# The down weights and the copy of x to the output in 26 small transfers instead of two large ones

## The chip, the cores and the metric

One core of one Trainium2 chip runs the kernel. The metric is the device time of one execution in microseconds; several runs are given by their median. The core has five engines with programs of their own: TensorE (PE, with its weight loads as PEld), VectorE (DVE), ScalarE (ACT), GpSimd (POOL) and SyncE (SP). SP and POOL issue the DMA transfers of this kernel; 16 DMA engines carry them out.

## The reference, cut to what matters

```python
xn = layernorm(x)                            # x: 2048 x 640, bf16
qkv = xn @ wqkv                              # 32 heads of 20
s = (softmax(q k^T / sqrt(20)) v) @ wo       # all 2048 x 2048 scores of each head
g = silu((sigmoid(xn @ w_gate) * (xn @ w_up)) @ w_down)   # 640 -> 1728 -> 640
out = x + s * g
```

The attention branch needs 32 x 2048 x 2048 exponentials. The gated branch is three matrix products with a hidden width of 1728 (13 tiles of 128 columns and one of 64).

## The kernel before, in words

**Setup (L160 to L361).** x is loaded, normalised and transposed into `xnT`; the first tiles of K, Q and V are made.

**Main loop (L1194 to L1246).** The queries go in NQC = 4 chunks of 512, the heads in NG = 8 groups of 4. A pass is one chunk with one group; there are 32. A pass has PER_PASS = 64 banks: a bank is 128 keys of one head against the 512 queries, one score matmul (L1035) of 512 columns. ACT takes the exponentials of two or three banks at once (`act_exp`, L1058); a fourth bank of a round can go to DVE, which builds the exponential by a cubic (`dve_exp`, L1069 to L1082). The products with V (L1167) gather in the PSUM tile `oacc`.

**The order of the work** is not found on the chip. The Python program keeps a clock `pe[0]` and estimated clocks of ACT and DVE, and writes the instructions in the order in which these say they should go. Each engine then takes its instructions in that order and waits on semaphores where an input is not there. `front()` is the first bank not yet issued on some lane.

**Fillers.** Between the rounds PE does the rest of the work in small jobs, sorted by a due bank (L829 to L861) and at most two in flight (L927): Q, K and V products, gate and up products (`gateup_job`, one for each of the 14 hidden tiles and each chunk), down products (`down_job`, 4 for each chunk, which read the weights `wd`, here `glu[1]`, and end in a silu), output products (`out_job`, 4 for each of the first three chunks) and the last chunk's (`part_job`). A job yields "known" (a condition tested while the program is written), "wait", "bank" (a PSUM bank) or "mm". Where there is room and no job, PE multiplies by zeros (L1146).

**Denominators.** At the end of each pass `normalise` copies `oacc` with DVE (L770), and POOL writes the four rows of sums to DRAM (L771) and reads them back over 128 partitions (L776). DVE takes the reciprocal (L780), POOL writes it (L781) and reads it back spread (L787), and DVE multiplies (L799). These small transfers are issued by POOL.

**Transfers on SP.** SP carries the weights of the gate and up products (L619, L621; two buffers each, one load of 160 KB each for a job), the projected Q on its way to DRAM and back (L550, L588, L608), the output weights in 32 small pieces (`load_wo`), and what the change is about: `start_glu` (L878), which runs once the K and V jobs are done and their weights' memory is free. It opens the memory for the gated branch, loads the first gate and up weights, then `wd` (L886, and L887 for the last 64 rows), then copies the first 12 of the 16 row tiles of x to the output in DRAM (L889). `out_job` later adds its result to that copy with an accumulating DMA of POOL (L726).

Of the kernel before, what the change touches and what calls it, by code (L numbers as in the profile page):

```python
# [15 lines left out]
P = 128  # L16
HEAD = 32
GH = 4
NG = HEAD // GH
QC = 512  # L20
# [24 lines left out]
def kernel(  # L45
# [11 lines left out]
    nc = tc.nc  # L57
# [6 lines left out]
    F = B_w_gate.shape[1]  # L64
    NFT = (F + P - 1) // P
    fsz_list = [min(P, F - i * P) for i in range(NFT)]
    TT = S // P
    NQC = S // QC
# [6 lines left out]
    x_view = x2.rearrange("(p t) d -> p t d", t=TT)  # L75
    out_view = out2.rearrange("(p t) d -> p t d", t=TT)
# [296 lines left out]
    DMA_WAIT, LANDED = 3400.0, 4000.0  # L373
# [36 lines left out]
    pe = [0.0]  # L410
# [254 lines left out]

    def down_job(tt):
        c, t4 = divmod(tt, QC // P)
        yield "known", lambda: (len(h_cells.get(c, [])) == NFT and (tt < 2 or tt - 2 in gq_cells)
                                and (c < NQC - 1 or front() >= PER_PASS * (NG * c + t4 + 1)))
        yield "wait", h_cells[c] + ([gq_cells[tt - 2]] if tt > 1 else [])  # L670
        hT = hTs[c]
        d2 = glu[0].tile([P, D], FP32, tag="d2", bufs=2, name="d2")
        got = []
        for h in range(2):
            e0_, e1_ = h * HALF, (h + 1) * HALF
            held, psd = yield "bank",
            for kf in range(NFT):
                fsz = fsz_list[kf]
                nc.tensor.matmul(psd[:, 0:HALF], lhsT=hT[0:fsz, kf, t4 * P:(t4 + 1) * P],  # L679
                                 rhs=glu[1][0:fsz, kf, e0_:e1_], start=(kf == 0), stop=(kf == NFT - 1))  # L680
                yield "mm", MM3
            got.append(dve.add(400.0, [Cell(pe[0] + PE_OUT)], lambda psd=psd, e0_=e0_, e1_=e1_:
                               nc.vector.tensor_copy(out=d2[:, e0_:e1_], in_=psd[:, 0:HALF]), 1))
            give_bank(held, got[-1])
        d_cells.setdefault(c, []).append(Cell(pe[0]))
        made = {}

        def tanh():
            made["t"] = glu[0].tile([P, D], BF16, tag="td", bufs=1, name="td")
            nc.scalar.activation(out=made["t"], in_=d2, func=ACT.Tanh, scale=0.25)  # L690

        def finish():
            last = c == NQC - 1
            gq = kT_all[:, t4, :].bitcast(FP32)[:, 0:D] if last else d2
            nc.vector.scalar_tensor_tensor(out=gq, in0=made["t"], scalar=1.0, in1=d2, op0=ALU.add, op1=ALU.mult)
            if last:
                gq_last[t4] = gq
            else:
                nc.gpsimd.dma_start(out=gq_dram[tt, :, :], in_=d2)

        turned = act.add(590.0, got + td_free[-1:], tanh, 0, EXP_LAG)
        td_free.append(dve.add(740.0, [turned], finish, 2))
        gq_cells[tt] = td_free[-1]
# [2 lines left out]

    def out_job(tt):
        qc, t4 = divmod(tt, QC // P)
        yield "known", lambda: all((qc, g) in ot_cells for g in range(NG)) and (not tt or tt - 1 in out_cells)
        yield "wait", [ot_cells[qc, g] for g in range(NG)] + ([out_cells[tt - 1]] if tt else [])  # L710
        gqr = glu[0].tile([P, D], FP32, tag="gqr", bufs=4, name="gqr")
        nc.sync.dma_start(out=gqr, in_=gq_dram[tt, :, :])
        landed = Cell(pe[0] + 3000.0)
        for h in range(2):
            held, pss = yield "bank",
            for g in range(NG):
                nc.tensor.matmul(pss[:, 0:HALF], lhsT=oTs[qc, g][:, t4 * P:(t4 + 1) * P],  # L717
                                 rhs=wo_pad[:, g, h * HALF:(h + 1) * HALF], start=(g == 0), stop=(g == NG - 1))
                yield "mm", MM3

            def finish(h=h, pss=pss):
                half = gqr[:, h * HALF:(h + 1) * HALF]
                nc.vector.scalar_tensor_tensor(out=half, in0=pss[:, 0:HALF], scalar=0.25, in1=half,
                                               op0=ALU.mult, op1=ALU.mult)
                if h == 1:
                    nc.gpsimd.dma_start(out=out_view[:, tt, :], in_=gqr, accum_op=ALU.add)  # L726

            done = dve.add(400.0, [Cell(pe[0] + PE_OUT), landed], finish, 1)
            give_bank(held, done)
        out_cells[tt] = done  # L730
# [80 lines left out]
    K_COST, B_COST = 5 * MM5, 0.3 * MM5  # L811
    GU_COST, DOWN_COST = 10 * MM5, 2 * NFT * MM3
    OUT_COST, PART_COST = 2 * NG * MM3, 2 * (NG - 2) * MM3
    WO_FROM = 2
    K_DUE, Q_DUE, B_DUE, V_DUE, OUT_DUE = -60, -50, -36, 6, 4 * PER_PASS

    class Job:
# [45 lines left out]
    glu = []  # L863
# [6 lines left out]
    def load_wo():  # L870
        if next_wo[0] == HEAD or front() < PER_PASS * WO_FROM + 8 * next_wo[0]:
            return
        h = next_wo[0]
        g, j = divmod(h, GH)
        nc.sync.dma_start(out=wo_pad[32 * j + 1:32 * j + 1 + Dh, g, :], in_=A_wo[h * Dh:(h + 1) * Dh, :])
        next_wo[0] += 1

    def start_glu():  # L878
        early.close()
        gp = ctx.enter_context(tc.tile_pool(name="glu", bufs=2, side="right", reuse_waits="tile"))  # L880
        wd = gp.tile([P, NFT, D], BF16, tag="wd", bufs=1, name="wd")
        glu.extend([gp, wd])
        for kf in range(WB - 1):
            load_glu(0, kf)
        nf = F // P
        nc.sync.dma_start(out=wd[:, 0:nf, :], in_=B_w_down[0:nf * P, :].rearrange("(f p) d -> p f d", p=P))  # L886
        nc.sync.dma_start(out=wd[0:F - nf * P, nf, :], in_=B_w_down[nf * P:F, :])  # L887
        ahead_of = (NQC - 1) * QC // P
        nc.sync.dma_start(out=out_view[:, 0:ahead_of, :], in_=x_view[:, 0:ahead_of, :])  # L889

    flight = []

# [100 lines left out]
    def front():  # L993
        return min(bank_of(j) for j in range(GH))
# [199 lines left out]
    while pv_pass[0] < len(steps):  # L1194
        advance(pe[0])
        pads()
        load_wo()
        ci, b0 = chunk[0], at_bank[0]
        p = min(b0, NB - 1) // PER_PASS
        until, stuck, can = 1e18, False, False  # L1200
        if b0 < NB:
            wanted = lacks()
            late = [w[2] for w in wanted if w[0].get(w[1]) is None]
            if late:
                must_fill(max(min(late) - 1, 0))
                continue
            cells = [w[0][w[1]] for w in wanted] + [sets[ci % 2]]
            stuck = any(c.t is None for task in act.queue for c in task[3])
            guess = pe[0] + (2000.0 if stuck else 400.0)
            free = max(c.t if c.t is not None else guess for c in cells)  # L1210
            dry = max(act.t, pe[0]) + sum(t[2] for t in act.queue) - MM5 - PE_OUT + 2000.0 * stuck
            into = 0.0 if mode[0] == "score" else INTO["score"]
            until = max(free, dry - AHEAD) - into
            can = all(c.t is not None for c in cells) and free <= pe[0] + into + 1.0
            if can and (until <= pe[0] + (0.0 if mode[0] == "score" else 40.0) or idle):
                idle = False
                n = issue()
                credit = min(credit + n * per_bank(b0), 3000.0)
                continue
        room = until - pe[0]  # L1220
        next_round[0] = until
        held = sum(len(q) for q in ready_p)
        batch = pv_batch()
        cost = PV_TIME + (INTO["pv"] if mode[0] != "pv" else 0.0)
        if batch and (cost <= room or held >= HELD):
            pv(batch)
            idle = False
            continue
        least = (0.0 if mode[0] == "fill" else INTO["fill"]) + MM3
        hurry = (b0 >= NB or stuck or any(x.due < b0 + URGENT for x in flight + jobs[:1])  # L1230
                 or held >= 12 and lacks_v())
        if (credit > 0.0 or hurry) and least <= room:
            took = fill(p, room)
            if took:
                credit -= took
                idle = False
                continue
        if b0 < NB and can and not idle:
            idle = True
            continue  # L1240
        if zero_add(room):
            idle = False
            continue
        soon = [q[k][1].made.t for q in ready_p for k in range(min(2, len(q)))]
        times = [until, pe[0] + 150.0] + [t + SEM for t in soon if t is not None]
        pe[0] = min(t for t in times if t > pe[0] + 1.0)  # L1246
# [83 lines left out]
```

## Time and profile before

| what | value |
|---|---|
| runs | 903.64, 906.02, 906.61 us (median 906.02) |
| profiled execution | 904.48 us |
| its span in the profile | 902.7 us |
| ACT busy | 871.1 us (96%) |
| DVE busy | 840.9 us (93%) |
| PE busy | 824.4 us (91%) |
| POOL busy | 162.2 us (18%) |
| DMA traffic | 64.38 MB, mean 71 GB/s |
| large transfers | `wd` 2080.0 KB and 80.0 KB, x to output 1920.0 KB, one each |

The span is the stretch that the profile covers, from the first to the last instruction; the execution's own time lies 1.8 us above it. A line of the profile's groups reads: line, engine, operation, written tile <- read tiles, shapes, count, busy time and mean of one, and the idle time of the engine just before with what ended most of it. In a timeline row the start and the length come first, and the idle time before stands in brackets at the end. In a row of stretches each engine's busy time has its count of instructions in brackets; behind the engines come the clock that TensorE was granted (1.00 is full), the mean busy share of the DMA engines and what they moved. Landing is the time from the issue of a DMA to the arrival of its last data.

### The profile page before, as it was taken

How to read it: one execution, taken by the hardware profiler on the slowest of the kernel's cores; microseconds unless marked ns; L12 is line 12 of the kernel's file. 1: busy time of each engine (PE TensorE's matmuls, PEld its weight loads, DVE VectorE, ACT ScalarE, POOL GpSimd, SP SyncE). 2: the span in 40 equal slices, each digit the busy share in tenths (PEclk: the TensorE clock that was granted, in tenths of full speed). 3: DMA queues.
4: the chain of work that ended last, by engine and by line, in shares of the span. 5: the costliest groups of instructions: out<-in, count | busy, mean ns of one | idle time of the engine just before them, and what ended most of it. 6: DMA issues, size and time to landing. Idle time of an engine off the chain costs nothing.

```text
span 902.7 us, 16725 instructions
## 1 busy us (share of the span) xinstructions
PE 824.4 (91%) x6190; PEld 288.9 (32%) x6190; DVE 840.9 (93%) x1484; ACT 871.1 (96%) x837; POOL 162.2 (18%) x305
## 2 busy tenths in 40 slices
PE   5899999989999999999999999999999999999995
PEld 3334333322223333232233332232332322233332
DVE  7799999989999999997999999999999989899994
ACT  6999999998999999999999999999999999999992
POOL 7401111101111212111101221101121221011120
PEclk9999999998999999999999999999999999999997
DMA  8112231255321134323202343303022432200021
GB/s 314 45 40 83 71 100 35 65 191 139 72 70 41 55 92 68 70 58 72 63 23 78 88 70 69 75 23 81 27 70 65 106 63 66 56 19 13 13 58 44
DMA packets 105895, 64.38 MB, mean 71 GB/s; under 512 B 79982, under 2 KB 100002, under 8 KB 105594
## 3 DMA queue, kind: packets, MB, share of 16 engines
q1 hardware_dynamic: 95606, 47.21, 19.3%
q0 software_dynamic: 10208, 16.11, 8.0%
q8 instruction: 48, 0.79, 0.4%
q14 instruction: 33, 0.27, 0.1%
HBM read 50.45 MB, written 16.13 MB: 74 GB/s over the span
## 4 chain that ended last, share of the span: by engine, by line
ACT 62%; issue 18%; PE 11%; DVE 7%; DMA 1%; SPq 0%; POOL 0%; DVEq 0%; ACTq 0%; POOLq 0%
ACT p L1058 57%; PE sc L1035 4%; ACT tnh L650 3%; PE oacc L1167 2%; DVE dy L1069 1%; PE work L643 1%; DVE du L1074 1%; PE work L123 1%; PE work L679 1%; ACT td L690 1%; DVE stats L226 1%; PE work L656 1%; DMA den<-den_dram 1%; DVE p L1082 1%; DVE du L1078 1%
## 5 line engine op out<-in xcount | busy, mean ns | idle before, releaser
L1058 ACT ACTIVATE p<-sc 128x1536 bf16<-128x1536 f32 x717 | 828.2, 1357 | 6.4 <-PE spare L1035 2.4
L1035 PE MATMUL sc<-qT,kT_all 21*128 21x512 bf16 x1791 | 280.5, 383 | 49.2 <-ACT p L1058 42.3
L1069 DVE TENSOR_SCALAR dy<-spare 128x512 f32<-128x512 f32 x257 | 175.9, 685 | 24.0 <-PE spare L1035 21.2
L1035 PEld LDWEIGHTS <-kT_all 21*128 21x128 bf16 x2048 | 90.1, 91 | 289.2 <-issue 277.5
L1078 DVE SCALAR_TENSOR_TENSOR du<-du,dy 128x512 f32<-128x512 f32 x257 | 174.7, 683 | 1.6
L1082 DVE SCALAR_TENSOR_TENSOR p<-du,dy 128x512 uint16<-128x512 f32 x257 | 174.5, 682 | 1.3
L1074 DVE SCALAR_TENSOR_TENSOR du<-dy 128x512 f32<-128x512 uint16 x257 | 174.8, 684 | 0.8
L1167 PE MATMUL oacc<-p,v_all 128*21 128x512 bf16 x2048 | 157.8, 385 | 0.3 <-DVE v_all L156 0.3
L1035 PE MATMUL spare<-qT,kT_all 21*128 21x512 bf16 x257 | 99.0, 385 | 2.4 <-DVE row L584 2.4
L771 POOL DMA_DIRECT2D den_dram<-oev x31 | 18.0, 580 | 389.6 <-DVE oev L770 389.6
L679 PE MATMUL work<-wd,hT 128*128 128x320 bf16 x448 | 85.5, 302 | 0.1
L643 PE MATMUL work<-xnT,wg 128*128 128x512 bf16 (+1 forms) x280 | 81.2, 383 | 0.4
L656 PE MATMUL work<-xnT,wu 128*128 128x512 bf16 (+1 forms) x280 | 76.1, 385 | 0.4
L1146 PE MATMUL oacc<-xnT,zero 128*128 128x512 bf16 x227 | 75.2, 384 | 0.6 <-DVE oev L770 0.6
L787 POOL DMA_DIRECT2D rl<-rec_dram x124 | 61.7, 503 | 62.9 <-DMA rec_dram<-den 53.4
L679 PEld LDWEIGHTS <-hT 128*128 128x128 bf16 x448 | 35.0, 97 | 48.6 <-issue 39.1
L1167 PEld LDWEIGHTS <-v_all 128*21 128x21 bf16 x2048 | 29.4, 90 | 65.1 <-issue 63.5
L650 ACT ACTIVATE tnh<-work 128x512 bf16<-128x512 f32 (+1 forms) x56 | 41.1, 733 | 0.0
L660 DVE SCALAR_TENSOR_TENSOR hT<-tnh,work 128x512 bf16<-128x512 bf16 (+1 forms) x56 | 38.0, 679 | 2.6 <-ACT tnh L650 1.9
L781 POOL DMA_DIRECT2D rec_dram<-den x31 | 17.0, 548 | 124.9 <-DVE den L780 120.4
L717 PE MATMUL work<-wo_pad,oT 128*128 128x320 bf16 x192 | 35.6, 302 | 0.0
L643 PEld LDWEIGHTS <-wg 128*128 128x128 bf16 (+1 forms) x280 | 21.7, 98 | 43.0 <-issue 32.2
(111 smaller groups left out, 553.9 us busy)
## 6 DMA issues: line engine op xcount, KB each, us to landing
wg<-in_B_w_gate_dram SPq DMA_DIRECT2D x52, 160.0 KB
wu<-in_B_w_up_dram SPq DMA_DIRECT2D x52, 160.0 KB
rl<-rec_dram POOLq DMA_DIRECT2D x124, 64.0 KB, 2.4
qT<-q_dram SPq DMA_DIRECT2D x31, 128.0 KB
gq_dram<-d POOLq DMA_DIRECT2D x12, 320.0 KB, 2.5
gqr<-gq_dram SPq DMA_DIRECT2D x12, 320.0 KB
kT_all<-k_dram SPq DMA_DIRECT2D x28, 128.0 KB
wd<-in_B_w_down_dram SPq DMA_DIRECT2D x1, 2080.0 KB
```

The lines of the kernel that those rows point to most:

```text
L643: nc.tensor.matmul(psg[0:fsz, :], lhsT=wg[:, kd, 0:fsz], rhs=xnT[:, kd, cols], start=(kd == 0), stop=(kd == KD - 1))
L650: nc.scalar.activation(out=made["t"][0:fsz, :], in_=psg[0:fsz, :], func=ACT.Tanh, scale=0.5)
L656: nc.tensor.matmul(psu[0:fsz, :], lhsT=wu[:, kd, 0:fsz], rhs=xnT[:, kd, cols], start=(kd == 0), stop=(kd == KD - 1))
L679: nc.tensor.matmul(psd[:, 0:HALF], lhsT=hT[0:fsz, kf, t4 * P:(t4 + 1) * P], rhs=glu[1][0:fsz, kf, e0_:e1_], start=(kf == 0), stop=(kf == N ...
L1035: nc.tensor.matmul(ps, lhsT=kT_all[32 * j:32 * j + 1 + Dh, g, kt * P:(kt + 1) * P], rhs=qTs[qc, g][32 * j:32 * j + 1 + Dh, :], start=True, ...
L1058: nc.scalar.activation(out=buf.tile(), in_=ps, func=ACT.Exp, bias=EXP_BIAS, scale=exp_scale)
L1069: nc.vector.tensor_scalar(out=t["y"], in0=ps, scalar1=LEAST, scalar2=None, op0=ALU.max)
L1074: nc.vector.scalar_tensor_tensor(out=t["u"], in0=t["f"], scalar=CUBE_2, in1=t["f"], op0=ALU.add, op1=ALU.mult)
L1078: nc.vector.scalar_tensor_tensor(out=t["u"], in0=t["u"], scalar=CUBE_1, in1=t["f"], op0=ALU.add, op1=ALU.mult)
L1082: nc.vector.scalar_tensor_tensor(out=buf.tile()[:, 0, :].bitcast(U16), in0=t["u"], scalar=CUBE_SCALE, in1=t["y"], op0=ALU.mult, op1=ALU.add)
L1146: nc.tensor.matmul(oacc, lhsT=zero, rhs=xnT[:, 0, 0:QC], start=not begun, stop=not begun, skip_group_check=True)
L1167: nc.tensor.matmul(oacc[32 * j:32 * j + 1 + Dh, :], lhsT=v_all[:, b % PER_PASS // GH, GH * g + j, 0:1 + Dh], rhs=buf.ap[:, i, :], start=(n ...
```

## The change

`start_glu` still loads the first gate and up weights, and then only notes how far the scores are. A new function, called once in each turn of the main loop, issues one transfer whenever `front()` has moved on by six banks: first the 14 tiles of the down weights, one by one (160 KB, the last 80), then 12 row tiles of x to the output (160 KB each). The first down job is not begun before all 14 tiles are issued and the last of these transfers, of either kind, is 4000 ns old by the program's clock; an output job is not begun before its row tile's copy is issued.

```diff
     def down_job(tt):
-        yield "known", lambda: (len(h_cells.get(c, [])) == NFT and (tt < 2 or tt - 2 in gq_cells)
+        yield "known", lambda: (bulk[0] == NFT and pe[0] > bulk_t[0] + LANDED and len(h_cells.get(c, [])) == NFT and (tt < 2 or tt - 2 in gq_cells)
                                 and (c < NQC - 1 or front() >= PER_PASS * (NG * c + t4 + 1)))
...
     def out_job(tt):
-        yield "known", lambda: all((qc, g) in ot_cells for g in range(NG)) and (not tt or tt - 1 in out_cells)
+        yield "known", lambda: (bulk[1] > tt and all((qc, g) in ot_cells for g in range(NG))
+                                and (not tt or tt - 1 in out_cells))
...
-    WO_FROM = 2
+    WO_FROM, BULK_EVERY, bulk_t = 2, 6, [0.0]
...
         for kf in range(WB - 1):
             load_glu(0, kf)
-        nf = F // P
-        nc.sync.dma_start(out=wd[:, 0:nf, :], in_=B_w_down[0:nf * P, :].rearrange("(f p) d -> p f d", p=P))
-        nc.sync.dma_start(out=wd[0:F - nf * P, nf, :], in_=B_w_down[nf * P:F, :])
-        ahead_of = (NQC - 1) * QC // P
-        nc.sync.dma_start(out=out_view[:, 0:ahead_of, :], in_=x_view[:, 0:ahead_of, :])
+        glu_from.append(front())
+
+    glu_from, bulk = [], [0, 0]
+    XT = (NQC - 1) * QC // P
+
+    def load_bulk():
+        if not glu_from or sum(bulk) == NFT + XT or front() < glu_from[0] + BULK_EVERY * (1 + sum(bulk)):
+            return
+        if bulk[0] < NFT:
+            kf = bulk[0]
+            fsz = fsz_list[kf]
+            nc.sync.dma_start(out=glu[1][0:fsz, kf, :], in_=B_w_down[kf * P:kf * P + fsz, :])
+            bulk[0] += 1
+        else:
+            tt = bulk[1]
+            nc.sync.dma_start(out=out_view[:, tt, :], in_=x_view[:, tt, :])
+            bulk[1] += 1
+        bulk_t[0] = pe[0]
...
         load_wo()
+        load_bulk()
```

## The prediction on record

> **What bounds the kernel now.** I read the page first, for the engine that is never free, then its time by stretches, then the one stretch that stands out.
>
> ```profile
> span 902.7 us, 16725 instructions
> ...
> ACT 62%; issue 18%; PE 11%; DVE 7%; DMA 1%; SPq 0%; POOL 0%; DVEq 0%; ACTq 0%; POOLq 0%
> ...
> L1058 ACT ACTIVATE p<-sc 128x1536 bf16<-128x1536 f32 x717 | 828.2, 1357 | 6.4 <-PE spare L1035 2.4
> L1035 PE MATMUL sc<-qT,kT_all 21*128 21x512 bf16 x1791 | 280.5, 383 | 49.2 <-ACT p L1058 42.3
> ```
>
> ACT leads the chain that ended last, and its exponentials at L1058 fill 828.2 of 902.7 us. The order of work on each engine is fixed when the program is written, so an idle microsecond of ACT is a microsecond of the span unless ACT idles later anyway. PE waits for ACT (42.3 us in front of L1035), not ACT for PE. So I look for ACT's idle time. The columns behind the width of a stretch are PE, PEld, DVE, ACT and POOL busy, then granted clock, DMA share, GB/s.
>
> ```profile
> 168.00:196.00 28.00, 26.47 (x196) 8.89 (x198) 27.20 (x51) 28.00 (x26) 3.74 (x8) 1.00 0.33 94
> 196.00:224.00 28.00, 24.93 (x158) 6.80 (x156) 22.88 (x41) 23.62 (x23) 3.63 (x7) 0.88 0.66 205
> 224.00:252.00 28.00, 25.93 (x186) 8.05 (x184) 25.83 (x43) 28.00 (x29) 3.69 (x7) 1.00 0.33 75
> ```
>
> ACT is full on both sides and short by 28.00 - 23.62 = 4.38 us in one stretch, where the DMA share doubles and the clock falls. In steps of 2 us:
>
> ```profile
> 198.00:200.00 2.00, 1.94 (x10) 0.49 (x7) 1.04 (x4) 2.00 (x3) 0.00 (x0) 1.00 1.06 365
> 200.00:202.00 2.00, 0.51 (x4) 0.10 (x4) 0.00 (x0) 2.00 (x4) 0.00 (x0) 1.00 1.15 405
> 202.00:204.00 2.00, 1.08 (x9) 0.12 (x8) 1.84 (x4) 0.82 (x1) 0.55 (x1) 0.61 1.06 440
> 204.00:206.00 2.00, 2.00 (x13) 0.53 (x6) 1.90 (x4) 0.90 (x1) 0.00 (x0) 0.50 0.95 340
> 206.00:208.00 2.00, 2.00 (x11) 0.38 (x13) 0.53 (x2) 0.23 (x2) 0.00 (x0) 0.50 0.90 208
> ```
>
> DVE stops first (0.00 from 200 to 202), then PE, then ACT; the clock halves last. The timelines say why. SP's, then POOL's (start, length, what; in brackets the idle time before and what ended it):
>
> ```profile
> 192.48 0.54 SPq L886 DMA_DIRECT2D wd<-in_B_w_down_dram  x1
> 193.07 1.56 SPq L887 DMA_DIRECT2D wd<-in_B_w_down_dram  x1
> 194.68 0.97 SPq L889 DMA_DIRECT2D out_dram<-in_A_x_dram  x1
> ```
>
> ```profile
> 192.13 0.57 POOL L771 DMA_DIRECT2D den_dram<-oev  x1 [12.89 <-DVE oev L770]
> 195.95 0.57 POOL L776 DMA_DIRECT2D den<-den_dram  x1 [3.24 <-DMA den_dram<-oev]
> ```
>
> L886 and L889 are the two large transfers (2080 and 1920 KB, issued 2.2 us apart). Behind them the small read of the denominators, issued at 195.95, is late. Then DVE's, PE's and ACT's:
>
> ```profile
> 202.08 0.25 DVE L780 RECIPROCAL den<-den 128x16 f32<-128x16 f32 x1 [3.04 <-DMA den<-den_dram]
> ```
>
> ```profile
> 202.92 0.58 PE L1035 MATMUL spare<-qT,kT_all 21*128 21x512 bf16 x1 [2.41 <-DVE row L584]
> ```
>
> ```profile
> 205.10 1.02 ACT L1058 ACTIVATE p<-sc 128x1024 bf16<-128x1024 f32 x1 [2.28 <-PE sc L1035]
> 207.90 2.53 ACT L1058 ACTIVATE p<-sc 128x1536 bf16<-128x1536 f32 x2 [1.77 <-PE spare L1035]
> 210.70 1.45 ACT L1058 ACTIVATE p<-sc 128x1536 bf16<-128x1536 f32 x1 [0.27 <-PE spare L1035]
> ```
>
> DVE, which takes its work in order, stands 3.04 us in front of the reciprocal (from 199.04); the bank that PE wants is emptied by DVE behind it (L584), so PE stands 2.41 us; ACT runs out of scores (2.28 us); then PE works at half clock and ACT waits another 1.77 + 0.27 us. Sum for ACT: **4.32 us**, nearly the whole 4.38.
>
> **The change part by part.** *The burst goes: -4.32 us.* Whether it goes whole depends on the read of the denominators landing before DVE asks. The landings of this line, before 191 us and after 212 us:
>
> ```profile
> DMA to landing us min/median/max: 1.9/2.0/2.7
> ```
>
> ```profile
> DMA to landing us min/median/max: 1.8/2.2/3.8
> ```
>
> Without the burst the read can issue at about 192.13 + 2.2 = 194.3 (an estimate, a small write taking as long as the read's median). DVE asks at 199.04: 4.7 us of room against at most 3.8. Even DVE late by 3.04 - 2.28 = 0.76 us would not reach ACT, by the way the one wait became the other. What is late next is nothing: ACT is full again from 212 us on.
>
> *26 transfers come.* One every six banks. How far that reaches is counted from the score matmuls issued so far (PE busy with their count, then weight loads, for L1035 alone):
>
> ```profile
> 0.00:192.48 192.48, 55.28 (x396) 17.67 (x396) 1.00 0.29 92
> 0.00:232.00 232.00, 67.86 (x478) 21.13 (x478) 0.99 0.35 107
> 0.00:264.00 264.00, 78.11 (x554) 24.76 (x555) 0.99 0.35 103
> 0.00:289.90 289.90, 86.64 (x618) 27.37 (x618) 0.99 0.34 99
> ```
>
> From 396 banks, the 14th piece goes at 396 + 84 = 480 (232 us) and the 26th at 396 + 156 = 552 (264 us): one piece per 71.5 / 26 = 2.75 us. (156 banks are 2.4 passes of 64.) What a 160 KB piece holds of the 16 DMA engines is bounded by two rows, the burst and a pair of 160 KB weight loads:
>
> ```profile
> 192.00:208.00 16.00, 13.52 (x78) 3.44 (x80) 10.82 (x23) 11.95 (x12) 1.70 (x3) 0.83 1.01 326
> 231.00:234.00 3.00, 3.00 (x22) 0.80 (x20) 2.07 (x4) 3.00 (x4) 0.20 (x1) 1.00 0.51 115
> 228.00:264.00 36.00, 33.67 (x238) 10.44 (x235) 33.48 (x56) 36.00 (x37) 6.23 (x12) 1.00 0.31 70
> ```
>
> 163.8 kB at the burst's 326 GB/s are 0.50 us; the pair held 3.00 x 0.51 = 1.53 us, so 0.77 us each. All 26 take 13 to 20 us, which lifts the stage's share from 0.31 by 0.18 to 0.28: about half, where the burst had 1.01. I take 0.6 us and no cost. It is hidden under ACT's exponentials as long as the gate and up weights come in time; the rows of one pair:
>
> ```profile
> 230.24 0.37 SPq L619 DMA_DIRECT2D wg<-in_B_w_gate_dram  x1
> 231.32 0.38 SPq L621 DMA_DIRECT2D wu<-in_B_w_up_dram  x1
> ```
>
> ```profile
> 239.03 0.61 PE L643 MATMUL work<-xnT,wg 128*128 128x512 bf16 x2
> ```
>
> L619 waits for the weights of the job before the last, so these are used two jobs on, at 239.03; the pair was through by 234. That is 5.0 us of room; two pieces ahead take 1.5. Cost: 0 (a gain is excluded, nothing waits for these loads now; the loss beyond the room is rival C).
>
> *SP issues 26 DMAs for three.* At 0.37 (L619) to 0.54 us (L886) that is 9.6 to 14.0 us against 0.54 + 1.56 + 0.97 = 3.07, over 71.5 us in which SP mostly waits for buffers. Behind a piece on SP stand weight loads, and q_dram and qT transfers: each is delayed by at most 0.54 us, against the 5.0. Cost 0.
>
> *Two added conditions.* The first down job asks that all 14 pieces are issued and the last bulk transfer is 4 us old; the copies of x renew that time stamp too, so the gate opens only at about 264 + 4 = 268 us. The job could not start before anyway:
>
> ```profile
> 290.14 0.57 PE L679 MATMUL work<-wd,hT 128*128 128x320 bf16 x3
> ```
>
> That leaves 22 us. The output jobs, gated on their copy of x, come later still (they are not admitted before pass 9). So I expect **the same order of work as before, bank for bank**. PE's waits for 14 pieces instead of two are for data 58 us old: a few semaphore instructions on an engine that waits for ACT 42.3 us in all. Cost 0, at worst a few tenths of PE's slack.
>
> *Sum.* -4.32 + 0 + 0 + 0. The profiled execution took 904.48 us, 1.54 under the median of 906.02 (903.64 to 906.61). All four known executions have a mean of 905.2; less 4.3 that is 900.9. I say **901.0 us**, and a span of 902.7 - 4.3 = 898.4.
>
> The Trainium skill (DMA: Bandwidth & Descriptors, Bandwidth) speaks against the change: it advises transfers of at least 1 MiB, and fits 2.0 us plus bytes at 436 GB/s to one DMA of POOL's path. By that, as an estimate, a piece is 2.4 us and all 26 are 62 us; the pair above, at 0.77 us each of the engines' time, does not bear it out as a time that holds the queue.
>
> **The rivals.** *B, part of the stall stays.* Pieces and weight loads meet the read of the denominators, as SP lets two or three pieces out together after a wait (its longest in this stage is below, under 2.75 x 3). With three pieces ahead, the read lands at 194.3 + 3.8 + 3 x 0.77 = 200.4, DVE waits 1.4 us, ACT 0.6 us, or 2.7 if PE's clock falls again (2.04 more). Time 901.6 to 903.7; with the whole stall kept, which is also the case that the spreading does not take place, 905.2.
>
> ```profile
> SPq L550 <- DVE dy L1069: 6.1, 1, 6.1
> ```
>
> For it: this chain has been late once. Against: the landings elsewhere, up to 3.8, and the 4.7 us of room. The Trainium skill (TensorE: Matmul & The Clock Gate, Part 1) puts half clock after an idle window of about 3.4 us; here the clock halved after a wait of 2.41 us behind a sparsely used PE (0.51 of 2.00 from 200 to 202), so the window is not a safe floor. By the page B costs 0.6, by the trace up to 2.7.
>
> *C, the other side: pieces are dearer than their bytes.* If each held the queue for a small transfer's landing (2.2 us, the median above) besides its 0.50, 26 x 2.7 + 0.31 x 71.5 = 92.4 us of work meets 71.5 us. The backlog of 20.9 us eats the weights' 5.0 of room; PE stands 15.9 us, ACT 15.9 - 0.76 + 2.04 = 17.2, net +12.9: 918.1. The point from which it decides is (1 - 0.31) x 71.5 / 26 = 1.9 us a piece; the rows say 0.50 to 0.77. By the Trainium skill's 2.4 us (the page on DMA named above) the same sum is a backlog of 12.6 us and +4.6 net, 909.8.
>
> *D, the order changes.* If the gate of the down jobs binds (the last piece later than 285 us, where my count says 264), chunk 1's jobs start later and everything behind them is placed anew. What that does is chiefly the number of score banks that DVE takes from ACT: a bank costs ACT 828.2 / 1791 = 0.46 us, so ten banks more or fewer are 4.6 us either way: 896.3 to 905.6.
>
> **How the numbers follow.** About 0.3%, 2.7 us, is what a measurement of this kernel can tell from no change: faster means below 903.3, slower above 908.7. Forecast 0.72 (898.5 to 903.5, from 903.64 - 4.3 = 899.3 and 906.61 - 4.3 = 902.3 with a microsecond on either side), B 0.12, C 0.06, D 0.10. Faster: 0.68 of the forecast, 0.03 of B, 0.04 of D, 0.75. Slower: all of C and 0.02 of D's worst, 0.08. Same: 0.17. For 8 in 10 the range takes the forecast's own, the lower half of B and the middle of D: 898.5 to 905.0.
>
> **What would show each step.** Right: ACT 28.00 in the stretch around 196 to 224; clock 1.00 there; no wait of L780 for a DMA; the landing maximum of L776 under 4; 26 issues of at most 160 KB about 2.75 us apart on SP; ends of passes earlier by 4 to 5 us from pass 6 on; still 717 exponentials on ACT. Wrong: another count at L1058 (D); PE waiting for weights between 212 and 268 us (C); DVE still waiting at L780 (B); or ACT full where it was idle and idle somewhere new, which I have not seen coming.

## The result, and the profile after

| | before | after |
|---|---|---|
| median of the runs | 905.19 us (4 runs, 903.64 to 906.61) | 899.93 us (4 runs, 899.43 to 900.52) |
| profiled execution | 904.48 us | 899.65 us |
| its span | 902.7 us | 897.9 us |

The ratio is 0.9943, with a 95% interval of 0.9923 to 0.9962: faster by 0.57%, against 901.0 us forecast. The order of the instructions on PE, ACT, DVE and POOL is the same in both programs, line by line; only SP's differs.

The page of after, its groups with the lines shown of before. Line numbers shift with each edit (here by 14, in `normalise` by one); the operation and the tiles tell which row is which.

```profile
L1072 ACT ACTIVATE p<-sc 128x1536 bf16<-128x1536 f32 x717 | 828.2, 1362 | 2.0 <-PE oacc L1181 1.4
L1049 PE MATMUL sc<-qT,kT_all 21*128 21x512 bf16 x1791 | 279.8, 382 | 56.9 <-ACT p L1072 48.5
```

The count of exponentials and their busy time are the same; the idle time in front of them fell from 6.4 to 2.0 us. PE's idle time in the second line can't be set against that of before (49.2, of it 42.3 for ACT): the profile of after lacks the records of 84 of the 6190 matmuls, and a missing record counts as idle time. The profile of e1 below lacks as many and has 48.6 us there at the time of before; that of e5 has all, and 42.1. The stretches of after that answer to the gap:

```profile
196.00:224.00 28.00, 25.66 (x186) 8.01 (x181) 27.36 (x47) 28.00 (x28) 4.18 (x8) 1.00 0.52 138
224.00:252.00 28.00, 25.89 (x179) 8.33 (x179) 25.69 (x43) 28.00 (x29) 3.67 (x7) 1.00 0.50 127
```

ACT is full where it had 23.62 of 28.00, the clock is whole, the DMA share is about a half for two stretches. The denominators of the same pass in after, POOL's and DVE's timelines:

```profile
195.94 0.57 POOL L777 DMA_DIRECT2D den<-den_dram  x1 [3.35 <-DMA den_dram<-oev]
```

```profile
198.86 0.24 DVE L781 RECIPROCAL den<-den 128x16 f32<-128x16 f32 x1
```

The reciprocal has no wait any more. Its read is issued no earlier than before, though. Where the time came from is seen from the copies that end a pass, DVE's timeline of before, then of after:

```profile
191.16 0.68 DVE L770 COPY oev<-oacc 128x512 f32<-128x512 f32 x1
221.98 0.69 DVE L770 COPY oev<-oacc 128x512 f32<-128x512 f32 x1
...
862.49 0.68 DVE L770 COPY oev<-oacc 128x512 f32<-128x512 f32 x1
```

```profile
191.05 0.69 DVE L771 COPY oev<-oacc 128x512 f32<-128x512 f32 x1
217.09 0.68 DVE L771 COPY oev<-oacc 128x512 f32<-128x512 f32 x1
...
857.58 0.68 DVE L771 COPY oev<-oacc 128x512 f32<-128x512 f32 x1
```

After was 0.11 us ahead before the stage, 4.89 behind it, and 4.91 at the last such copy. All of the gain falls into one pass, and nothing is given back later.

### The profile page after: what moved, and what is told of

The parts are those of the page before. It is cut to its first block, busy times and chain, and to the rows that moved or that the text cites. A ratio compares the mean times of both kernels' runs of the same rounds, so it can differ in the third digit from the quotient of the medians.

```text
span 897.9 us, 16669 instructions
## 1 busy us (share of the span) xinstructions
PE 806.3 (90%) x6106; PEld 289.3 (32%) x6190; DVE 840.6 (94%) x1484; ACT 870.7 (97%) x837; POOL 161.6 (18%) x305
## 3 DMA queue, kind: packets, MB, share of 16 engines
q1 hardware_dynamic: 97382, 47.21, 19.8%
## 4 chain that ended last, share of the span: by engine, by line
ACT 64%; issue 18%; PE 10%; DVE 7%; DMA 0%; SPq 0%; ACTq 0%; DVEq 0%
ACT p L1072 59%; PE sc L1049 3%; ACT tnh L650 3%; PE oacc L1181 2%; DVE dy L1083 1%; PE work L643 1%; DVE du L1088 1%; PE work L123 1%; PE work L679 1%; ACT td L690 1%; DVE stats L226 1%; DVE p L1096 1%; DVE du L1092 1%; PE work L149 1%; DMA x_sb<-in_A_x_dram 0%
## 5 line engine op out<-in xcount | busy, mean ns | idle before, releaser
L643 PE MATMUL work<-xnT,wg 128*128 128x512 bf16 (+1 forms) x261 | 77.6, 383 | 2.0 <-issue 0.8
L656 PE MATMUL work<-xnT,wu 128*128 128x512 bf16 (+1 forms) x268 | 73.1, 381 | 1.2 <-DVE dy L1083 0.3
L1160 PE MATMUL oacc<-xnT,zero 128*128 128x512 bf16 x175 | 59.1, 384 | 3.7 <-issue 2.9
L679 PEld LDWEIGHTS <-hT 128*128 128x128 bf16 x448 | 35.0, 97 | 48.6 <-issue 39.1
```

Source lines behind the costliest of these rows:

```text
L643: nc.tensor.matmul(psg[0:fsz, :], lhsT=wg[:, kd, 0:fsz], rhs=xnT[:, kd, cols], start=(kd == 0), stop=(kd == KD - 1))
L656: nc.tensor.matmul(psu[0:fsz, :], lhsT=wu[:, kd, 0:fsz], rhs=xnT[:, kd, cols], start=(kd == 0), stop=(kd == KD - 1))
```

## The experiments

All but the third, the sixth, the eighth and the eleventh have the order of before on PE, ACT, DVE and POOL. e3 and e6 differ from it on DVE alone. Each ratio is against runs of the kernel before that were taken beside it (medians 904.45 us for e1 to e4, 904.26 for e5 to e8, 905.43 for e9 to e12), over all runs, so it is not the quotient of two medians of the table. "ACT idle" is what ACT lacks in the profiled execution's stretches from 196 to 252 us.

| run | median us | ratio (95%) | profiled us | ACT idle us | profiled less idle |
|---|---|---|---|---|---|
| before | 905.19 | | 904.48 | 4.38 | 900.1 |
| after | 899.93 | 0.9943 (0.9923 to 0.9962) | 899.65 | 0.00 | 899.7 |
| e1 copy whole | 904.40 | 1.0000 (0.9986 to 1.0015) | 903.98 | 3.94 | 900.0 |
| e2 weights whole | 903.38 | 0.9982 (0.9969 to 0.9995) | 903.70 | 3.10 | 900.6 |
| e3 reciprocal later | 906.81 | 1.0020 (1.0008 to 1.0031) | 907.09 | 6.97 | 900.1 |
| e4 26 at once | 910.25 | 1.0059 (1.0043 to 1.0076) | 910.61 | 10.10 | 900.5 |
| e5 weights first | 903.62 | 0.9986 (0.9971 to 1.0001) | 906.42 | 6.52 | 899.9 |
| e6 both sheltered | 906.92 | 1.0025 (1.0007 to 1.0043) | 909.24 | 8.36 | 900.9 |
| e7 26 behind weights | 906.63 | 1.0028 (1.0012 to 1.0043) | 906.91 | 6.94 | 900.0 |
| e8 every 12 banks | 899.35 | 0.9940 (0.9925 to 0.9955) | 898.62 | 0.00 | 898.6 |
| e9 four of 1 MB | 899.43 | 0.9937 (0.9924 to 0.9951) | 899.57 | 0.00 | 899.6 |
| e10 every 2 banks | 900.22 | 0.9944 (0.9929 to 0.9958) | 900.32 | 0.07 | 900.2 |
| e11 every 9 banks | 900.26 | 0.9947 (0.9933 to 0.9960) | 900.76 | 0.00 | 900.8 |
| e12 every 12, gate on weights | 900.21 | 0.9946 (0.9932 to 0.9959) | 900.29 | 0.00 | 900.3 |

The last column is the point of the table: take ACT's idle time of this one stage away, and every kernel takes 898.6 to 900.9 us. The profiled executions differ by what ACT loses between 196 and 252 us, and by next to nothing else.

### Half the burst: e1 and e2

```diff
# e1: the copy whole at the start, the weights in pieces
+        nc.sync.dma_start(out=out_view[:, 0:XT, :], in_=x_view[:, 0:XT, :])
+        bulk[1] = XT
         glu_from.append(front())
...
-        if not glu_from or sum(bulk) == NFT + XT or front() < glu_from[0] + BULK_EVERY * (1 + sum(bulk)):
+        if not glu_from or bulk[0] == NFT or front() < glu_from[0] + BULK_EVERY * (1 + bulk[0]):
# e2: the weights whole (as L886, L887 of before) with bulk[0] = NFT, the copy in pieces
```

> The changed kernel, but the copy of x goes in one transfer of 1920 KB at the start of the stage; the down weights stay in 14 pieces. PE, ACT, DVE and POOL have the order of both kernels. Theory (a threshold): half the burst, 1.97 MB, is through in some 6 us at the 326 GB/s seen before, by about 199; the read of the denominators lands when DVE asks (198.9) or less than 0.8 us later, which ACT does not feel. So ACT loses under 0.5 us there and the time is that of the changed kernel, 899.5 to 900.8. Rival (every megabyte costs its share): half the gain is gone, 902 to 903.

> The changed kernel, but the down weights go in two transfers (2080 and 80 KB) at the start of the stage; the copy of x stays in 12 pieces. The order on PE, ACT, DVE and POOL is that of both kernels. Theory (a threshold): as with the copy alone, 2.2 MB are through by about 199.5, DVE waits under 0.8 us, ACT under 0.5 us: 899.5 to 900.8. Rival (share by megabyte): 902 to 903. If only one of the two transfers makes the stall, this run and the one with the whole copy differ by 4 us or more.

Neither held: both medians lie above the rival's range too. Either half alone keeps most of the loss: no gain with the copy whole, 0.18% with the weights whole. The timeline of e1, DVE's wait and then ACT's:

```profile
201.83 0.25 DVE L781 RECIPROCAL den<-den 128x16 f32<-128x16 f32 x1 [2.63 <-DMA den<-den_dram]
```

```profile
204.85 1.02 ACT L1074 ACTIVATE p<-sc 128x1024 bf16<-128x1024 f32 x1 [1.89 <-PE sc L1051]
207.65 2.45 ACT L1074 ACTIVATE p<-sc 128x1536 bf16<-128x1536 f32 x2 [1.77 <-PE sc L1051]
210.37 1.45 ACT L1074 ACTIVATE p<-sc 128x1536 bf16<-128x1536 f32 x1 [0.27 <-PE spare L1051]
```

The read of the denominators lands after 5.9 us in e1 and 5.9 in e2, against 6.1 in before: with half the bytes in the queue it is nearly as late. My picture, that the read waits in proportion to what is queued, fell. So did the rival's "a share for each megabyte".

### Another victim: e3

```diff
# RECIP_LATE = 3300.0, by the program's clock
         def s2():
-            nc.vector.reciprocal(out=t["den"], in_=t["den"])
-            nc.gpsimd.dma_start(out=rec_dram[n, :, :].rearrange("j (r c) -> (j r) c", c=GH * QC // P), in_=t["den"])
+            def turn():
+                nc.vector.reciprocal(out=t["den"], in_=t["den"])
+                nc.gpsimd.dma_start(out=rec_dram[n, :, :].rearrange("j (r c) -> (j r) c", c=GH * QC // P), in_=t["den"])
+
+            if n == 5:
+                at(dve.t + RECIP_LATE, turn)
+            else:
+                turn()
             at(dve.t + DMA_WAIT, s3)
```

> The kernel before with its three large transfers, but in the pass of the burst DVE takes five other instructions (3.1 us of them) ahead of the reciprocal, so that it does not stand waiting for the denominators, which land at about 202.05. Nothing else moves on PE, ACT, POOL and SP. Theory A (the prediction's: the late read of the denominators is the whole cost): no stall, 900 to 901. Theory B (the burst has a second victim behind it): the gate weights of the second hidden tile, issued on SP behind the copy at 195.7, land only when the queue is empty, about 208, and PE, no longer held up, asks for them at about 204; PE waits 3 to 4 us for a DMA at the gate product, ACT loses 2 to 5 us, and the time stays at 903 to 906.

This was meant to tell whether the late denominators are the whole cost. DVE no longer waits for them, and the kernel is **slower** than before, by 0.20%. PE's timeline in e3, then ACT's:

```profile
208.88 0.61 PE L643 MATMUL work<-xnT,wg 128*128 128x512 bf16 x1 [4.60 <-DMA wg<-in_B_w_gate_dram]
```

```profile
211.41 1.45 ACT L1064 ACTIVATE p<-sc 128x1536 bf16<-128x1536 f32 x1 [5.32 <-PE spare L1041]
...
215.92 4.62 ACT L1064 ACTIVATE p<-sc 128x1536 bf16<-128x1536 f32 x4 [1.65 <-PE sc L1041]
```

Theory B holds: the second hidden tile's gate weights stand on SP behind the copy of x. The profile of before has no such wait, because PE, held up by the wait for the denominators, came to this product at about the same time and found the weights there; PE's timeline of before:

```profile
209.23 1.04 PE L643 MATMUL work<-xnT,wg 128*128 128x512 bf16 x4
```

One wait hid a longer one.

### All 26 at once: e4

```diff
-    WO_FROM, BULK_EVERY, bulk_t = 2, 6, [0.0]
+    WO_FROM, BULK_EVERY, bulk_t = 2, 0, [0.0]
...
         glu_from.append(front())
+        for _ in range(NFT + XT):
+            load_bulk()
```

> All 26 pieces of the changed kernel, issued one behind the other at the start of the stage: the size is that of after, the timing that of before. The order on PE, ACT, DVE and POOL is the same. Theory (it is the spacing that helps): the burst and its stall come back, ACT idle 4 to 6 us between 200 and 212, 904 to 907. Rival (it is the size: small transfers let others in between): 900 to 901.

The spacing is what helps, and cutting without it is worse than before (910.25 us), worse even than the 904 to 907 us expected. SP's timeline in e4, then PE's:

```profile
192.86 6.86 SPq L899 DMA_DIRECT2D wd<-in_B_w_down_dram  x14
199.77 7.87 SPq L903 DMA_DIRECT2D out_dram<-in_A_x_dram  x12
207.69 0.58 SPq L619 DMA_DIRECT2D wg<-in_B_w_gate_dram  x1
```

```profile
212.24 0.61 PE L643 MATMUL work<-xnT,wg 128*128 128x512 bf16 x1 [7.69 <-DMA wg<-in_B_w_gate_dram]
```

Issuing 26 pieces takes SP 14.8 us, and the gate weights are not even issued before 207.69 (195.71 in before). The denominators came sooner, after 3.8 us instead of 6.1: DVE waited 0.66 us and ACT stood only behind the weights. Of the 7.69 us that PE waited, 3.1 had passed before SP got the weights issued.

### One victim sheltered after the other: e5, e6, e7

```diff
# e5: the three large transfers behind the second tile's weights; e6: that and e3's edit
         glu_w[c, kf] = (wg, wu)
+        if (c, kf) == (0, 1):
+            load_all()
# e7: the 26 pieces at that place, with BULK_EVERY = 0 and no load_bulk() in the main loop
         glu_w[c, kf] = (wg, wu)
+        if (c, kf) == (0, 1):
+            for _ in range(NFT + XT):
+                load_bulk()
```

> The kernel before, its three large transfers kept together, but issued on SP behind the gate and up weights of the second hidden tile instead of ahead of them; the reciprocal stays where it was. PE, ACT, DVE and POOL have the order of before. Theory (two waits side by side, each enough for the whole loss): the denominators are as late as before, 5.5 to 6 us from issue, DVE waits 2.5 to 3 us, PE some 2, ACT loses 3.5 to 4.5 us, no wait for gate weights: 903.5 to 905. Rival (the weights are the wait that counts, now that they are seen): 900 to 901.5.

> Both at once: the three large transfers stay together, behind the second hidden tile's weights, and DVE takes five instructions ahead of the reciprocal of that pass. Theory (the two waits are all that the burst costs; the bytes as such cost nothing): ACT loses under 0.7 us between 196 and 224, 899.5 to 901.5, the gain of the change without spreading anything. Rival (the burst hurts whatever stands behind it, the third tile's weights next, which are asked for at about 210): PE waits at the gate product of the third tile for 1 to 4 us and the time is 902 to 905.

> The 26 pieces at once, as in the earlier run, but behind the second hidden tile's weights. The reciprocal is where it was. Theory: the denominators land in some 3.8 us as in that run, DVE waits about 0.7 us or less, which ACT does not feel; the third tile's weights are issued only at about 208 and asked for at 210.4, so PE waits 0 to 1.5 us; ACT loses under 1 us: 899.5 to 901.5. Rival (all at once is the fault, whatever the order on SP): ACT loses 4 us or more, 904 to 910.

e5 came out as expected: its median is within the range given, the weights are no longer waited for, and DVE's wait for the denominators (2.26 us, a little under the 2.5 expected) stands first. Its profiled execution took 2.8 us more than the median and ACT lost 6.52 us in it, more than the 4.5 expected, with a mean clock of 0.76 in the stretch from 196 to 224 against 0.88 in before. In e7 the rival was right, in e6 only in part: the burst hurt what stood behind it, but the victim was not the third tile's weights (PE waited 0.24 us for them), and 906.92 us is above the rival's 905. The timeline of e6, DVE, then PE, then ACT:

```profile
214.75 0.69 DVE L807 TENSOR_TENSOR oT<-oev,rl 128x512 bf16<-128x512 f32 x1 [4.51 <-DMA rl<-rec_dram]
```

```profile
217.43 1.01 PE L658 MATMUL work<-xnT,wu 128*128 128x512 bf16 x2 [4.31 <-DVE dy L1080]
```

```profile
220.04 1.02 ACT L1069 ACTIVATE p<-sc 128x1024 bf16<-128x1024 f32 x1 [4.94 <-PE spare L1046]
```

The reciprocals' way back to SBUF (`rl`) is late now, from the write and the read that follow the displaced reciprocal, and DVE stands in front of the multiplication. The write took 5.4 us to land and the reads 3.7 to 4.4, against 1.9 and 2.1 to 3.6 in after. That DVE takes the reciprocal later has a part in it, which is not shown apart: no run has that edit without the burst. In e7 it is the third tile's gate weights, issued at 211.5 behind 26 pieces; PE's timeline, then ACT's:

```profile
214.38 2.31 PE L646 MATMUL work<-xnT,wg 128*128 128x512 bf16 x5 [3.98 <-DMA wg<-in_B_w_gate_dram]
```

```profile
217.33 1.02 ACT L1075 ACTIVATE p<-sc 128x1024 bf16<-128x1024 f32 x1 [5.12 <-PE spare L1052]
```

So four different transfers take the role in turn: the denominators, the second tile's weights, the reciprocals, the third tile's weights. Moving one out of the way uncovers the next.

### How much spacing: e9, e10, e12

```diff
# e9: 7 + 7 tiles of the weights, 6 + 6 of the copy
+        n = 7 if bulk[0] < NFT else 6
+        if front() < glu_from[0] + BULK_EVERY * (sum(bulk) + n):
+            return
# e10
-    WO_FROM, BULK_EVERY, bulk_t = 2, 6, [0.0]
+    WO_FROM, BULK_EVERY, bulk_t = 2, 2, [0.0]
# e12: BULK_EVERY = 12, and bulk_t[0] = pe[0] only behind a piece of the weights
```

> The pace of after (160 KB per six banks) in large pieces: the down weights in two transfers of seven tiles (the last with its 64 rows apart), the copy of x in two of six, 960 to 1120 KB each, 36 to 42 banks apart. PE, ACT, DVE and POOL have the order of before and after. Theory (what hurts is a backlog of 6 us and more in the queue; a transfer of 1.1 MB is through in some 3.4 us at 326 GB/s, and weights and denominators have about that to spare): ACT loses under 0.7 us in the stage, 899.5 to 901.5. Rival (any transfer longer than a piece that meets the denominators' chain or a pair of weights stalls): 902 to 904.5, with a DVE or PE wait for a DMA behind one of the four.

> The changed kernel with a piece every 2 banks instead of 6: all 26 within 52 banks, some 21 us, a piece every 0.8 us where a piece takes about 0.6 of all 16 engines. The order on the four engines is the same. Theory (no backlog as long as a piece is done before the next comes): DMA share about 0.9 from 194 to 214, ACT loses under 1 us, 899.5 to 901.5. Rival (with the weights and denominators beside them the engines are full, and a backlog builds as at once): 903 to 907, a wait for gate weights or denominators of 2 us or more.

> A piece every 12 banks, but the time stamp that the down jobs look at is renewed by pieces of the down weights alone. PE, ACT, DVE and POOL have the order of before and after again. Theory (ACT has nothing left to lose in the stage with a piece every 6 banks, so halving the pace brings nothing): 899.4 to 900.6, the time of after; what the earlier run with 12 banks had below that came from its order, one bank more on DVE. Rival (pieces every 6 banks still cost): 898.5 to 899.3.

All three give the gain whole. The pieces may come in a third of the banks (e10, its stretch first; SP issues them within 28.5 us there and within 65.6 in after), and they may be seven times as large (e9) if they stand apart:

```profile
196.00:224.00 28.00, 25.81 (x186) 7.70 (x186) 26.93 (x47) 27.93 (x28) 4.26 (x8) 1.00 0.74 198
```

DVE's waits from 190 to 300 us, of e10 and then of e9:

```profile
DVE den L781 <- DMA den<-den_dram: 0.8, 1, 0.8
```

```profile
DVE den L781 <- DMA den<-den_dram: 1.0, 2, 0.8
```

Both come near an edge: DVE waits up to 0.8 us for the denominators, and ACT loses 0.07 us in e10 and nothing in e9. That agrees with the 0.76 us of tolerance that the prediction read off before; no run here has a wait just beyond it.

### The gate: e8 and e11

```diff
-    WO_FROM, BULK_EVERY, bulk_t = 2, 6, [0.0]
+    WO_FROM, BULK_EVERY, bulk_t = 2, 12, [0.0]     # e11: 9
```

> The changed kernel with a piece every 12 banks instead of 6: 26 pieces reach 312 banks on, to bank 708, and since the copies of x renew the time stamp, the first down job (bank 618 otherwise) waits for all of them. The order on all engines changes behind that point: 258 banks on DVE instead of 257, 716 exponentials on ACT instead of 717. Theory (the late gate costs PE only idle time that it has, and one bank more on DVE gives ACT 0.5 us): 898.5 to 901. Rival D of the prediction (a bound gate spoils the order): 902 to 906.

> The changed kernel with a piece every 9 banks: 26 pieces reach bank 396 + 234 = 630, about 4 us apart, so that the first down job (bank 618 otherwise) waits for the gate, if it does not slip through between two copies. The order behind it changes: 258 banks on DVE instead of 257. Theory: ACT stays full, 898.5 to 900.5. Rival D of the prediction (a bound gate spoils the order and costs): 902 to 906.

e8 has the time expected for another reason: 12 banks are about 5.5 us (156 were 71.5), more than the 4 us that the gate asks, so the gate opens between two copies and the first down product stands at 284.97 us, where it stands at 285.22 in after. Only later ones of the chunk are held back (a group at 318.29 us that after does not have), and with them the order changes. In e11, at 9 banks or about 4.1 us, the gate does bind from the start; PE's timeline:

```profile
295.86 0.85 PE L679 MATMUL work<-wd,hT 128*128 128x320 bf16 x5
```

The first down product is 10.6 us later than in after, the order behind it is another (716 exponentials on ACT, 258 banks on DVE), and the time is that of after. Among after, e8 and e9 to e12 the intervals overlap: none of them is shown to beat after.

## Why the prediction was right, point by point

- **What bounds the kernel.** Right. ACT's idle time in one stage accounts for all the runs within 1.2 us on either side of 899.7 (last column of the table), however it comes about.
- **-4.32 us for the stall.** The sign and the place were right, the size a little small: 4.78 us came out of that pass. 4.32 are the idle rows. Of the rest most is overlap: five exponentials, from the start of the one at 201.36 in before to the next tanh at 212.04, take 10.68 us; the same five take 5.79 in after (201.25 to 207.04). The difference is 4.89. Exponentials without a gap begin before their predecessor ends (1.34 us apart at 1.45 us long, in before's last one of the five); each gap loses that overlap too.
- **The late denominators as the cause.** Right as the wait that came first, wrong as the whole cost. "What is late next is nothing" is the sentence that failed for the burst: "ACT is full again from 212 us on" showed only that nothing else was late once PE had been held up. e3 shows the gate weights 4.60 us late once the denominators are out of the way. For the change itself it held, because spacing leaves nothing of the burst.
- **The read issued at 194.3, room 4.7 us.** Wrong. In after the write still takes 3.35 us beyond its issue and the read is issued at 195.94, as in before. The real room is 198.86 - 195.94 = 2.92 us, against landings of 2.2 to 2.5 us in the stage. The step was covered, but by 0.4 us and not by 0.9. Against the landing of 3.8 us that the prediction allowed for, 2.92 would have been 0.9 too little, a little more than the 0.76 that ACT does not feel; so that the stall went whole is in part luck.
- **A piece for 0.6 us.** About right. The queue that SP uses took 19.8% of 897.9 us in after and 19.3% of 902.7 in before, 3.6 us more for 26 pieces; in e12, with the same pieces, 0.9 more (19.5% of 898.1). That is 0.03 to 0.14 a piece above the burst's 0.50. The share came to 0.50 to 0.52, as estimated.
- **One piece every 2.75 us.** Nearly right on the mean (65.6 us for 25 intervals, 2.6 each), not singly: behind a wait SP lets up to four out together, which cost nothing.
- **The same order, bank for bank.** Right.
- **Rivals.** B did not occur. C's point (1.9 us a piece) is excluded by e10, where SP issues 26 pieces within 28.5 us and ACT loses 0.07. D's price was wrong where its case was made: in e11 the gate binds and the order is another, at no cost that can be measured. Whether the gate binds depends on the spacing too, not only on where the last piece falls: at 12 banks (5.5 us) it let the first down product through though the copies were not done, which I had not seen.

The Trainium skill's advice (DMA: Bandwidth & Descriptors, Bandwidth) to batch into transfers of 1 MiB and more neither helps nor hurts here: e9 nearly follows it at 899.43 us, after breaks it at 899.93, with overlapping intervals. The DMA engines' time that small pieces cost (0.9 to 3.6 us over the kernel) lies under ACT's work.

## What to carry to other kernels

A large transfer with no reader for 90 us is not free: it stands in a queue with transfers that have a reader in 3 us. Spread such bytes so that no backlog builds, and look at the distance between them before their size. When one wait is removed, ask what stands behind the same burst: here three more transfers were late, and the first wait hid them.

## What the runs showed of the hardware

**The clock falls in whole steps of time.** Stretches of before, set at the clock's edges:

```profile
201.00:202.40 1.40, 0.00 (x0) 0.00 (x0) 0.32 (x2) 1.40 (x2) 0.00 (x0) 1.00 1.03 409
202.40:209.20 6.80, 6.28 (x30) 1.15 (x29) 5.15 (x9) 2.75 (x3) 1.32 (x3) 0.50 0.91 292
209.20:211.00 1.80, 1.80 (x13) 0.60 (x11) 1.58 (x3) 1.47 (x3) 1.22 (x3) 0.99 0.66 139
```

and of e4:

```profile
207.00:208.70 1.70, 0.00 (x0) 0.00 (x0) 0.00 (x0) 0.00 (x0) 0.00 (x0) 0.99 0.81 236
208.70:218.90 10.20, 6.44 (x20) 1.74 (x21) 3.28 (x5) 2.85 (x3) 0.00 (x0) 0.50 0.58 152
218.90:220.00 1.10, 1.10 (x14) 0.21 (x11) 0.69 (x1) 0.68 (x1) 0.00 (x0) 1.00 0.02 4
```

Half clock lasts 6.8 us in one and 10.2 in the other, two and three times 3.4, and it begins while PE stands still. The Trainium skill (TensorE: Matmul & The Clock Gate, Part 1) has a free-running window of 3.4 us, and the trace agrees with that length. A wait of 2.41 us was enough here for two windows at half clock. The length of the wait does not set the number: a wait of 1.99 us in e2 went with one window (3.4 us), one of 1.64 us in e5 with four (13.7 us), in which PE was busy 13.3 us. So a stall has no fixed price: of the 6.46 us that e5's idle rows of ACT add up to, 4.95 come after the first row, as PE works at half clock. Among the executions of before beside e1 to e12, those with a mean clock of 0.994 or more took 903.1 to 904.3 us, those with 0.989 or less 906.0 to 907.6. What sets the number of windows is not settled.

**A small read behind a burst is late, but not in proportion to all that is queued.** The denominators' 8 KB landed 5.2 to 5.9 us after issue where one large transfer of 2.0 or 2.2 MB had been issued ahead (e1, e2, e5, e6), and 5.5 and 6.1 us where it was all 4.2 MB (e3, before): the second large transfer adds little. With fewer bytes issued ahead it is sooner: 3.8 us in e4, where SP had got seven of the 26 pieces out when the read was issued, 3.3 in e7 with five, 3.7 in e10 with three, 2.1 to 2.6 with one or two (after, e8, e11, e12), 1.8 in e9 with none. What sets the 5 to 6 us is not settled: no run changed the read itself or its queue.
